# Ordering a Conformer block by list scheduling on estimated times, with attention started on the first keys

## Chip, cores and metric

One NeuronCore of a Trainium2 chip runs the whole kernel. The metric is device time in microseconds (us). Each run also has a profile, whose span (first to last instruction) is some 2 to 3 us shorter than the device time of the same run. Stages below are in span time.

## The reference, cut to what matters

`B, T, D, K, H = 2, 4000, 144, 5, 4`, so a head has 36 elements. All inputs and the output are bf16.

```python
h = _silu(_layernorm(x) @ w_ff1a) @ w_ff1b           # 144 -> 576 -> 144
x = x + 0.5 * h
q, k, v = split(_layernorm(x) @ w_qkv)               # 4 heads of 36
att = softmax(q k^T * 36**-0.5) v                    # 4000 x 4000, full
x = x + att @ w_o
a, b = split(_layernorm(x) @ w_pw1);  h = a * _sigmoid(b)
c = sum over 5 taps of hp[:, i:i+T, :] * dw[i]       # depthwise, along T
x = x + _silu(c) @ w_pw2
h = _silu(_layernorm(x) @ w_ff2a) @ w_ff2b
return _layernorm(x + 0.5 * h)
```

## The kernel before

Tokens are cut into 16 chunks of 500 (8 for each batch), a chunk into 4 blocks of 125. The work of a chunk is a generator: `pre` (first feed-forward, then queries, keys and values), an attention epilogue, `post1` (output projection and gated linear unit) and `post2` (convolution, second feed-forward, final norm, store). Attention is 32 groups (batch, chunk of queries, pair of heads), each over 32 key tiles: 1024 exps of 125x1000 on ScalarE, each between score matmuls (`emit_S`) and output matmuls (`emit_O`). A program order for all engines is fixed when the kernel is built. Semaphores order the engines at run time, and an engine runs its own instructions in order, so a matmul that was placed too early holds every matmul behind it.

The order comes from three simple rules. The front drains all of `pre` for the first batch, four chunks at a time, before any attention; in attention a pump lets background generators go on by a token rate for each engine; the tail drains what is left.

```python
def ln(c, to_bf=True):                       # a norm works on the whole chunk
    s = yield from lnp.take()
    for i in range(NB):
        op("dve", "bn_stats", ST[0:TB, s, i, :], X[0:TB, c * NB + i, :], ...)
    yield
    for i in range(NB):
        op("dve", "bn_aggr", MV[0:TB, s, i, :], ST[0:TB, s, i, :], ...)
    op("pool", "tensor_scalar", RS[0:TB, s, :, 1], MV[0:TB, s, :, 1], LN_EPS, None, op0=ALU.add, ...)
    op("pool", "tensor_tensor", RS[0:TB, s, :, 0], RS[0:TB, s, :, 1], NHALF[0:TB, :], op=ALU.pow, ...)
    yield
    yield
    for i in range(NB):
        op("dve", "tensor_scalar", XN[0:TB, s, i, :], X[0:TB, c * NB + i, :], MV[...], RS[...], ...)
# ...
drain([pre(all_banks, 0, True), first()] + [pre(all_banks, c, True) for c in range(1, CPB)], 4)
bg = Banks([6, 7])                           # PSUM banks of the background during attention
pump = Pump({"pe": 0.35 * CLUMP, "dve": 0.75 * CLUMP, "act": 0.25 * CLUMP})
# ...
def post2_thread(b):                         # one chunk after the other
    for c in range(b * CPB, (b + 1) * CPB):
        while c not in u_done or (c + 1 < (b + 1) * CPB and c + 1 not in u_done):
            yield
        yield from post2(bg, c)
# ...
for n in range(len(its)):
    if n + 1 < len(its):
        emit_S(n + 1)
    emit_exp(n)
    release_held()                           # tanh gates, behind the exp
    emit_pending(n, 2)
    pend.append(n)
    if n % CLUMP == CLUMP - 1:
        pump.slot(cap=3)
# ...
drain(pump.threads, 8)
```

Silu is the ScalarE function only in the front. During attention and in the tail it is built from Tanh (ScalarE) and one multiply (VectorE), so that the function table of the exps stays loaded.

The softmax here doesn't subtract the row's maximum and nothing guards it: scores larger than these inputs give would overflow.

Of the kernel before, what the change touches and what calls it, by code (L numbers as in the profile page):

```python
# [23 lines left out]
class Op:  # L24
    __slots__ = ("eng", "name", "a", "k", "idx", "deps", "clock", "inc", "waits", "cnt", "q")


class Rec:



    ENGS = ("pe", "act", "dve", "pool", "sp")

    def __init__(self, nc):
        self.nc = nc
        self.ops = []
        self.n = {}
        self.hist = {}
        self.qs = {}
        self.cost = {e: 0.0 for e in self.ENGS}  # L40

    def op(self, eng, name, *a, r=(), w=(), q=None, cost=0.0, **k):
# [10 lines left out]
        for key in w:  # L53
            h = self.hist.setdefault(key, ([], []))
            o.deps += [(d, False) for d in h[0] + h[1] if d is not o]
            if h[1] and not (len(h[1]) == 1 and h[1][0] is o):
                self.hist[key] = ([o], [])
            else:
                h[0].append(o)
        self.ops.append(o)  # L60
        self.cost[eng] += cost
        return o

    def finish(self, group_qs=()):
        eng_clock = {e: {} for e in self.ENGS}
        qtotal = {l: n for l, n in self.n.items() if l.startswith("q:")}
        for o in self.ops:
            clk = eng_clock[o.eng]
            need = {}
            for d, raw in o.deps:  # L70
                lane = d.eng if d.q is None else "q:" + d.q
                if d.q is None and d.eng == o.eng and (d.eng == "pe" or not raw):
                    continue
                if d.q is None and d.eng == o.eng and o.q is not None:
                    continue
                if clk.get(lane, -1) >= d.idx:
                    continue
                if lane not in need or need[lane].idx < d.idx:
                    need[lane] = d
# [52 lines left out]
class Banks:  # L132
    def __init__(self, ids):
        self.free = list(ids)

    def take(self):
        while not self.free:
            yield
        return self.free.pop(0)

    def give(self, i):
        self.free.append(i)


def bass_standalone__conformer_family_zipformer__speech_kernel(
# [22 lines left out]
    op = R.op  # L168

# [3 lines left out]
    NS, NXT, NTH, NHT = 6, 5, 6, 3  # L173
    X = sb("X", [NBLK, D])
    XN = sb("XN", [NS, NB, D])
    ST = sb("ST", [NS, NB, 6], F32)
    MV = sb("MV", [NS, NB, 2], F32)
    RS = sb("RS", [NS, NB, 2], F32)
    NHALF = sb("NHALF", [NB], F32)
# [6 lines left out]
    NPT = 6  # L186
    OLAG = 3
    CLUMP = 2
# [4 lines left out]
    U = sb("U", [2, T + 4])  # L193
    SW = sb("SW", [2, 2, CH])
    IDENT = sb("IDENT", [128])
    IDF = sb("IDF", [128], F32)
    WA1 = sb("WA1", [2, FF])
# [21 lines left out]
    def load(eng, q, dst, src, w):  # L219
        op(eng, "dma_start", dst, src, q=q, w=w)  # L220
# [14 lines left out]
    load_x("sp", 1)  # L235
    load("act", "w1", WQKV[0:HD, :, :], kh(w_qkv), ["WQKV"])
    for c in range(2, CPB):
        load_x("sp", c)
    load("act", "w2", WO[0:HD, :, :], kh(w_o), ["WO"])
    load("act", "w2", WP1[0:HD, :, :], kh(w_pw1), ["WP1"])  # L240
    load("act", "w2", WP2[0:HD, :, :], kh(w_pw2), ["WP2"])
    load("act", "w2", DWR[0:KCONV, :], dw, ["DWR"])
    load_ff("act", "w2", WA2, WB2, w_ff2a, w_ff2b, "W2")
    for c in range(CPB, NCH):
        load_x("sp", c)

    op("pool", "memset", IDENT[:, :], 0.0, w=["ID0"])
# [3 lines left out]
    op("dve", "tensor_copy", IDF[:, :], IDENT[:, :], r=["ID"], w=["IDF"])  # L251
# [3 lines left out]
    op("dve", "memset", WB2[0:64, 4, :], 0.0, w=[("W2", "b", 2)])  # L255

    def setup_qk():
        for Wt, nm, o0 in ((WQ, "WQ", 0), (WK, "WK", D)):
            for k in range(2):
                op("dve", "tensor_copy", Wt[0:HD, k, :, 0:DH],  # L260
                   WQKV[0:HD, k, o0:o0 + D].rearrange("p (h d) -> p h d", h=H), r=["WQKV", nm + "0"], w=[nm])

    def va_init(b):
        blks = slice(b * NKT, (b + 1) * NKT)
        op("pool", "memset", VA[:, blks, :, DH + 1:64], 0.0, w=[("VA0", b)])
        op("pool", "memset", VA[:, blks, :, DH:DH + 1], 1.0, w=[("VA1", b)])

    va_init(0)
    va_init(1)
    op("pool", "memset", U[:, :, 0:2], 0.0, w=["U0"])  # L270
    op("pool", "memset", U[:, :, T + 2:T + 4], 0.0, w=["U0"])

    def setup_dw(banks):
        bk = yield from banks.take()
        for k in range(2):
            op("pe", "transpose", PSH[0:HD, bk, k * 8:k * 8 + KCONV], DWR[0:KCONV, k * HD:(k + 1) * HD],
               IDENT[0:KCONV, 0:KCONV], r=["DWR", "ID"], w=[("ps", bk)])
        yield
# [4 lines left out]
        yield  # L283
        for k in range(2):
            for i in range(KCONV):
                op("dve", "tensor_scalar", DG[0:HD, k, i, :], IDENT[0:HD, 0:HD], DWT[0:HD, k, i:i + 1], None,
                   op0=ALU.mult, r=["DWT", "ID"], w=["DG"])


    lnp, xtp, thp, htp, swp, anp = (Banks(range(n)) for n in (NS, NXT, NTH, NHT, 2, 2))  # L290

    def xkeys(c):
        return [("X", c, i) for i in range(NB)]

    def ln(c, to_bf=True):
        s = yield from lnp.take()
        for i in range(NB):
            op("dve", "bn_stats", ST[0:TB, s, i, :], X[0:TB, c * NB + i, :], r=[("X", c, i)], w=[("ST", s, i)],
               cost=0.25)
        yield  # L300
        for i in range(NB):
            op("dve", "bn_aggr", MV[0:TB, s, i, :], ST[0:TB, s, i, :], r=[("ST", s, i)], w=[("MV", s)], cost=0.12)
        op("pool", "tensor_scalar", RS[0:TB, s, :, 1], MV[0:TB, s, :, 1], LN_EPS, None, op0=ALU.add,
           r=[("MV", s)], w=[("VE", s)], cost=0.3)
        op("pool", "tensor_tensor", RS[0:TB, s, :, 0], RS[0:TB, s, :, 1], NHALF[0:TB, :], op=ALU.pow,
           r=[("VE", s), "NHALF"], w=[("RS", s)], cost=1.0)
        yield
        yield
        for i in range(NB):
            op("dve", "tensor_scalar", XN[0:TB, s, i, :], X[0:TB, c * NB + i, :], MV[0:TB, s, i, 0:1],  # L310
               RS[0:TB, s, i, 0:1], op0=ALU.subtract, op1=ALU.mult, r=[("X", c, i), ("MV", s), ("RS", s)],
               w=[("XN", s)], cost=0.14)
        yield
        return s

    def tr(banks, src, rk, free):

        s = yield from xtp.take()
        bk = yield from banks.take()
        dst = PSH[0:HD, bk, :].rearrange("p (k i n) -> p k i n", k=2, i=NB)  # L320
        for k in range(2):
            for i in range(NB):
                op("pe", "transpose", dst[:, k, i, 0:TB], src[:, i, k * HD:(k + 1) * HD], IDENT[0:TB, 0:TB],
                   r=[rk, "ID"], w=[("ps", bk)], cost=0.06)
        free()
        yield
        op("dve", "tensor_copy", XT[0:HD, s, :, :].rearrange("p k (i n) -> p k i n", i=NB), dst[:, :, :, 0:TB],
           r=[("ps", bk)], w=[("XT", s)], cost=0.6)
        banks.give(bk)
        yield  # L330
        return s

    def ln_tr(banks, c):
        s = yield from ln(c)
        return (yield from tr(banks, XN[0:TB, s, :, :], ("XN", s), lambda: lnp.give(s)))

    def residual(banks, c, mm, scale, rk, cost):

        for g in range(2):
            bk = yield from banks.take()  # L340
            for i in (2 * g, 2 * g + 1):
                terms = mm(i)
                for t, (l, rh) in enumerate(terms):
                    op("pe", "matmul", PSV[0:TB, bk, (i % 2) * D:(i % 2 + 1) * D], lhsT=l, rhs=rh, start=t == 0,
                       stop=t == len(terms) - 1, r=rk, w=[("ps", bk)], cost=0.06)
            yield
            ks = [("X", c, 2 * g), ("X", c, 2 * g + 1)]
            xa = X[0:TB, c * NB + 2 * g:c * NB + 2 * g + 2, :]
            op("dve", "scalar_tensor_tensor", out=xa, in0=PSV[0:TB, bk, 0:2 * D].rearrange("p (i d) -> p i d", i=2),
               scalar=scale, in1=xa, op0=ALU.mult, op1=ALU.add, r=[("ps", bk)] + ks, w=ks, cost=0.37)  # L350
            banks.give(bk)
        yield

    held = []
    hold = [False]

    def tanh_gate(bk, rows, done=None):
        t = yield from thp.take()

        def emit():  # L360
            op("act", "activation", TH[0:rows, t, :], PSV[0:rows, bk, 0:CH], ACT.Tanh, bias=0.0, scale=0.5,
               r=[("ps", bk)], w=[("TH", t)], cost=0.47)
            if done:
                done()

        if hold[0]:
            held.append(emit)
        else:
            emit()
        return t  # L370

    def release_held():
        while held:
            held.pop(0)()

    def ff(banks, c, s, WA, WB, nm, silu):
        h = yield from htp.take()
        pend = []

        def flush():  # L380
            if pend:
                bk, t, m = pend.pop(0)
                op("dve", "scalar_tensor_tensor", out=HT[:, h, m, :], in0=TH[:, t, :], scalar=1.0,
                   in1=PSV[:, bk, 0:CH], op0=ALU.add, op1=ALU.mult, r=[("TH", t), ("ps", bk)], w=[("HT", h)],
                   cost=0.6)
                banks.give(bk)
                thp.give(t)
# [326 lines left out]
```

## Time and profile before

| quantity | before |
|---|---|
| device time, median of 3 | 1250.53 us (1247.25 to 1250.77) |
| span of the profiled run, mean granted clock | 1247.4 us, 0.927 |
| front, until the first exp | 133.6 us |
| attention, first exp to the end of the last | 1042.2 us |
| tail, end of the last exp to the end | 71.6 us |

First the profile page of before: busy time, and the busy share in 40 slices of the span, in tenths. PEclk is TensorE's granted clock, in tenths of full speed.

```profile
PE 987.3 (79%) x10722; PEld 377.0 (30%) x10722; DVE 535.6 (43%) x1596; ACT 1041.1 (83%) x1250; POOL 109.2 (9%) x173
...
DVE  6567333444353544444434343434333333333354
ACT  2221799999999998999999998999999999999711
...
PEclk9756799999999998999999988999999999999855
```

ScalarE is at 90% or more only between the first slices and the last three; in those slices the clock is 0.5 to 0.9. Next, the same run by stage, the view of busy time in given stretches (start:end, length, busy us of each engine with its instructions, clock, DMA share, GB/s):

```profile
core 0: us, PE busy (x) PEld busy (x) DVE busy (x) ACT busy (x) POOL busy (x), PEclk, DMA share, GB/s
0.00:44.00 44.00, 23.53 (x132) 13.98 (x132) 24.90 (x91) 12.12 (x20) 13.03 (x21) 1.00 0.25 75
44.00:98.00 54.00, 46.02 (x230) 27.60 (x231) 34.71 (x123) 9.39 (x16) 10.10 (x16) 0.53 0.00 1
98.00:133.60 35.60, 28.08 (x147) 16.45 (x145) 27.36 (x85) 3.90 (x6) 5.04 (x8) 0.58 0.00 1
133.60:1176.00 1042.40, 851.70 (x10046) 297.25 (x10042) 412.10 (x1189) 1004.26 (x1189) 73.45 (x116) 0.98 0.01 3
1176.00:1247.40 71.40, 37.96 (x178) 21.68 (x178) 36.54 (x112) 11.46 (x20) 7.59 (x12) 0.54 0.02 7
```

In the front no engine is full, and TensorE runs at about half clock for two stretches, which makes its matmuls look busy for twice as long. (The 1.00 of the first row is not to be trusted: 18 wide matmuls from 28.15 us on took 7.71 us there, 0.43 each, which is the half-clock speed. The clock's record begins only at 38.7 us in this run. What lies before it counts as full clock in the listed means, so before's 0.927 is too high.) In attention ScalarE is the limit: an exp follows another after 0.895 us and a tanh takes 0.477 us of its time, so 1024 exps and 165 tanh are 916.5 + 78.7 = 995 us of the stage's 1042.2. The other 47 us I call stalls. 36 us of them are gaps that the trace lists. (0.895 is the mean over repeats with no listed gap between them; the median repeat is 0.884, so the border between work and stall is not sharp.)

One stall of attention in before's timeline (start, us, engine, operation, idle before it and its releaser):

```profile
423.42 0.68 DVE L121 TENSOR_TENSOR OTF<-PS,OTA 128x500 f32<-128x500 f32 x1
...
424.15 0.74 PEld L121 LDWEIGHTS PS<-IDF,OTF 128*125 128x125 f32 x4 [1.63 <-DVE OTF L121]
...
425.95 1.05 PE L121 MATMUL PS<-QT,KT 64*64 64x500 bf16 x8
...
426.63 1.90 ACT L121 ACTIVATE PT<-PS 125x1000 bf16<-125x1000 f32 x2 [2.04 <-PE PS L121]
```

The transposes of an epilogue stood in TensorE's order ahead of scores. They waited 1.63 us for VectorE's OTF; the scores behind them came late; the next exp waited 2.04 us. The wait is put down to TensorE, but it begins with an operand of VectorE. It is not the only cause: the granted clock was 0.50 from 424.4 to 427.8 us, so the transposes and the scores (8 in 1.05 us) were slow as well.

Finally the tail in before's chain of waits (the work that ended last, in order of time). Bare "PE PS" entries are merged matmuls.

```profile
1197.77 4.40 PE PS L121 x10
...
1202.81 0.68 DVE SW L121
...
1210.73 4.36 PE PS L121 x10
...
1223.21 1.18 DVE SW L121 x2
...
1231.63 4.36 PE PS L121 x10
```

The chain runs through the second half of `post2` twice: SW, the gated convolution, is ready for the one chunk at 1202.8 and for the other only at 1223.2, after the first chunk's whole second feed-forward. The 4.36 us entries are ten wide matmuls of 500 columns at half clock.

### The profile page before, as it was taken

The page shows a single profiled execution, that of the slowest core. Times are in us where ns is not written, and L with a number is a line of the kernel's source. Part 1 is how long each engine was busy: PE and PEld are TensorE (multiplying, and loading weights), DVE is VectorE, ACT ScalarE, POOL GpSimd, SP SyncE. Part 2 cuts the span into 40 slices and gives each one's busy share as a digit, 9 for nine tenths or more (in the row PEclk, how much of TensorE's full clock was granted, in tenths as well). Part 3 has the DMA queues.
Part 4 walks back from the last instruction along what each step waited for, and adds up shares of the span by engine and source line. Part 5 has one row for each costly group of instructions (what it writes and reads, how often), then busy time and mean ns, then how long its engine had stood idle before and what let it go on. Part 6 is the DMA issues. An engine that isn't in the chain of part 4 may idle for free.

```text
span 1247.4 us, 24613 instructions
## 1 busy us (share of the span) xinstructions
PE 987.3 (79%) x10722; PEld 377.0 (30%) x10722; DVE 535.6 (43%) x1596; ACT 1041.1 (83%) x1250; POOL 109.2 (9%) x173
## 2 busy tenths in 40 slices
PE   3888787878888888888877788887877777878754
PEld 2545222223232323233322232332322222222322
DVE  6567333444353544444434343434333333333354
ACT  2221799999999998999999998999999999999711
POOL 4121000000010100010000000000000000000011
PEclk9756799999999998999999988999999999999855
DMA  3000000000000000000000000000000000000000
GB/s 105 1 1 1 1 2 1 1 2 1 2 2 6 1 2 6 1 1 6 1 6 1 6 6 1 6 1 6 6 1 6 1 6 1 6 1 6 1 5 10
DMA packets 6430, 7.14 MB, mean 6 GB/s; under 512 B 1746, under 2 KB 6322, under 8 KB 6322
## 3 DMA queue, kind: packets, MB, share of 16 engines
q1 hardware_dynamic: 4160, 4.61, 1.1%
q8 instruction: 84, 1.38, 0.5%
q10 hardware_dynamic: 2162, 0.96, 0.3%
q14 instruction: 24, 0.20, 0.1%
HBM read 3.26 MB, written 2.30 MB: 4 GB/s over the span
## 4 chain that ended last, share of the span: by engine, by line
ACT 63%; PE 24%; DVE 9%; POOL 1%; issue 1%; DMA 1%; ACTq 0%; POOLq 0%; DVEq 0%
ACT PT L121 58%; PE PS L121 24%; ACT TH L121 5%; DVE OTF L121 2%; DVE OTA L121 2%; POOL RS L121 1%; DVE ST L121 1%; DVE XN L121 1%; DMA WB<-in_w_ff2b_dram 1%; DVE KT L121 1%; DVE VA L121 0%; DVE X L121 0%; ACTq L121 0%; DVE XT L121 0%; DVE MV L121 0%
## 5 line engine op out<-in xcount | busy, mean ns | idle before, releaser
L121 ACT ACTIVATE PT<-PS 125x1000 bf16<-125x1000 f32 x1024 | 949.4, 1059 | 51.0 <-PE PS L121 49.6
L121 PE MATMUL PS<-QT,KT 64*64 64x500 bf16 (+1 forms) x4096 | 412.3, 398 | 151.6 <-ACT PT L121 141.4
L121 PE MATMUL PS<-PT,VA 61*64 61x500 bf16 (+1 forms) x4096 | 385.4, 377 | 0.5 <-ACT PT L121 0.4
L121 PEld LDWEIGHTS PS<-QT,KT 64*64 64x64 bf16 (+1 forms) x4096 | 113.8, 104 | 532.3 <-ACT PT L121 495.5
L121 ACT ACTIVATE TH<-PS 128x500 bf16<-128x500 f32 (+1 forms) x184 | 115.9, 637 | 58.6 <-PE PS L121 57.6
L121 DVE SCALAR_TENSOR_TENSOR HT<-TH,PS 128x500 bf16<-128x500 bf16 x120 | 80.6, 674 | 146.5 <-ACT TH L121 146.5
L121 PEld LDWEIGHTS PS<-PT,VA 61*64 61x64 bf16 (+1 forms) x4096 | 119.9, 108 | 18.0 <-issue 4.7
L121 DVE SCALAR_TENSOR_TENSOR X<-PS,X 125x288 bf16<-125x288 f32 x128 | 58.5, 457 | 143.4 <-PE PS L121 143.1
L121 POOL TENSOR_SCALAR RS<-MV 125x4 f32<-125x4 f32 x80 | 18.4, 231 | 1126.4 <-DVE MV L121 1126.4
L121 DVE COPY XT<-PS 72x1000 bf16<-72x1000 bf16 x80 | 53.4, 676 | 140.9 <-PE PS L121 140.3
L121 PE MATMUL PS<-XT,WA 72*128 72x500 bf16 x320 | 107.0, 449 | 8.1 <-DVE HT L121 4.7
L121 DVE TENSOR_SCALAR XN<-X,MV,RS 125x144 bf16<-125x144 bf16 x320 | 79.4, 312 | 40.2 <-POOL RS L121 40.2
L121 ACT ACTIVATE HT<-PS 128x500 bf16<-128x500 f32 x40 | 22.8, 588 | 78.7 <-PE PS L121 78.7
L121 POOL TENSOR_TENSOR RS<-RS,NHALF 125x4 f32<-125x4 f32 x80 | 83.4, 1043 | 6.7
L121 DVE BATCH_NORM_STATS2 ST<-X 125x6 f32<-125x144 bf16 x320 | 76.4, 327 | 0.0
L121 PE MATMUL PS<-IDENT,XN 125*72 125x125 bf16 x512 | 47.3, 247 | 30.5 <-DVE XN L121 30.4
L121 PE MATMUL PS<-WB,HT 128*125 128x144 bf16 x640 | 60.3, 255 | 5.4 <-DVE HT L121 3.6
L121 PEld LDWEIGHTS PS<-WB,HT 128*125 128x125 bf16 x640 | 54.6, 161 | 21.7 <-issue 8.7
L121 PEld LDWEIGHTS PS<-IDENT,XN 125*72 125x72 bf16 x512 | 37.2, 130 | 51.2 <-DVE XN L121 34.8
L121 DVE SCALAR_TENSOR_TENSOR U<-TH,PS 72x500 bf16<-72x500 bf16 x32 | 32.3, 1009 | 43.3 <-ACT PT L121 27.0
L121 DVE COPY OTA<-PS 128x500 f32<-128x500 f32 x32 | 21.7, 679 | 64.7 <-PE PS L121 64.7
L121 PE MATMUL PS<-IDF,OTF 128*125 128x128 f32 x128 | 23.4, 307 | 29.4 <-DVE OTF L121 29.4
(46 smaller groups left out, 487.0 us busy)
## 6 DMA issues: line engine op xcount, KB each, us to landing
X<-in_x_dram SPq DMA_DIRECT2D x16, 140.6 KB
out_dram<-XN SPq DMA_DIRECT2D x16, 140.6 KB
WA<-in_w_ff1a_dram ACTq DMA_DIRECT2D x1, 162.0 KB
WA<-in_w_ff2a_dram ACTq DMA_DIRECT2D x1, 162.0 KB
WB<-in_w_ff1b_dram ACTq DMA_DIRECT2D x1, 144.0 KB
WB<-in_w_ff2b_dram ACTq DMA_DIRECT2D x1, 144.0 KB
WQKV<-in_w_qkv_dram ACTq DMA_DIRECT2D x1, 121.5 KB
WP<-in_w_pw_dram ACTq DMA_DIRECT2D x1, 81.0 KB
```

The costliest lines, as they stand in the source:

```text
L121: ins = getattr(eng, o.name)(*o.a, **o.k)
```

## The change

The intent is to use the same operations in a better order. Each recorded operation now has a cost, and the recorder keeps an estimated start and end for it. At each step the generator whose next piece can start first goes on (list scheduling), against the estimated start of the next scores. Attention begins as soon as all first feed-forwards of batch 0 and the keys of chunk 0 are done; the projections of chunks 1 to 7 run inside the first attention group. Norms, transposes and residuals work on half chunks. Silu is the ScalarE function in the front and, new, in the tail. 36 dummy matmuls run at the start to raise the clock. Two `post2` series run side by side. Smaller parts: U has a layout with a contiguous write (1.01 us before for one), at the price of 9 matmuls instead of 5 for one convolution half; value-tile clearing moves from large GpSimd operations to small VectorE ones (in before, VectorE's cast of an identity matrix took 7.11 us beside them; the Trainium skill, "SBUF — State Buffer", section "Who interferes with whom", says that a VectorE cast in one of its two-port modes and a GpSimd operation block each other; the trace fits, with 7.07 us of clearing on GpSimd beside the cast, but doesn't show the mode); the matrices for the convolution are made after the front and not at its start; ScalarE shares copies in front and tail; the late weights load from another queue; the output is stored in halves.

The diff, cut to its core (cuts are marked):

```diff
+    LAT = dict(pe=0.2, act=0.2, dve=0.12, pool=0.08, sp=2.0)
...
+        start = self.free[eng]
+        for d, raw in o.deps:
+            if d.eng != eng or d.q is not None or (raw and eng != "pe"):
+                start = max(start, d.done)
...
+        self.free[eng] = start + cost
+        o.done = start + cost + self.LAT[eng]
...
+class Sched:
+    def best(self, window=0.15):
+        c = [(self.start_of(th), th) for th in self.threads]
+        c = [(t, th) for t, th in c if t is not None]
...
+        lim = min(t for t, _ in c) + window
+        return next((t, th) for t, th in c if t <= lim)
...
+    NWARM = 36
+    for i in range(NWARM):
+        op("pe", "matmul", PSV[:, i % 8, 0:CH], lhsT=DUM[:, 0:128], rhs=DUM[:, 0:CH], ...)
...
-    def ln(c, to_bf=True):
-        s = yield from lnp.take()
-        for i in range(NB):
+    def ln(c, g):
+        u = yield need("dve", xnp)
+        for i in range(2):
...
-               out=U[0:HD, hf, 2 + cc * CH:2 + (cc + 1) * CH].rearrange("p (n i) -> p n i", i=NB),
+        op("dve", "scalar_tensor_tensor", out=U[0:HD, cc, hf, :, 1:1 + TB],
...
+        silu = mode["tail"]
+        kids = S.spawn(conv(c, z, hf, silu) for hf in range(2))
...
-    drain([pre(all_banks, 0, True), first()] + [pre(all_banks, c, True) for c in range(1, CPB)], 4)
+    while len(ff1_done) < CPB or 0 not in kv_done:
+        t, th = S.best()
+        S.run(th)
+    att_banks = set(range(6))
+    banks.restrict([6, 7])
...
+    while n_e < NIT:
+        a = s_start(n_s) if n_s < NIT else R.free["pe"]
+        t, th = S.best()
+        if th is not None and (a is None or t < a or (th.req[0] == "act" and t < a + 0.05)):
+            S.run(th)
+            if mode["front"] and len(kv_done) == CPB:
+                mode["front"] = False
+                S.add(setup_dw())
+                S.add(series(g for c in range(CPB, NCH) for g in (ff1(c, False), pre2(c))))
+                for par in range(2):
+                    S.add(series(post2(c) for c in range(par, NCH, 2)))
+            continue
+        if n_s < NIT:
+            emit_S(n_s)
+            n_s += 1
+        if n_s >= 2 or n_s == NIT:
+            emit_exp(n_e)
+            emit_pending()
...
-    drain(pump.threads, 8)
+    mode["tail"] = True
...
+    while S.threads:
+        t, th = S.best()
+        S.run(th)
```

## The prediction

> What bounds the kernel now. The timeline of ScalarE and the busy time by windows show three stages. Front, 0 to 133.6 us, until the first exp: ScalarE is busy 2 to 3 us in 10, VectorE 6; chunks go through their norms in lockstep, TensorE waits for VectorE and its granted clock falls to 0.50 from about 46 to 90 us and again later. Attention, 133.6 to 1176 us: ScalarE is the limit. An exp repeats every 0.895 us, a tanh takes 0.48 us of its time, so 1024 exps are 916 us and some 164 tanh 79 us; the other 47 us are stalls (ScalarE's listed gaps sum to 36 us, all released by TensorE). The long ones (2.0 us at 427, 2.4 at 495, 2.4 at 761) come where TensorE, in order, sat behind a background matmul whose VectorE operand was late; there the clock shows 0.50 too. Tail, 1176 to 1247 us: 71 us of one dependent chain for the last chunks, one after the other, clock about 0.5.
>
> What changes.
> 1. Front. Only the first feed-forward of eight chunks and chunk 0's keys must end before attention. By the order of instructions VectorE has about 43 us of work up to the first query copy, costed with the trace (statistics 0.22, aggregate 0.09, normalise 0.25, residual 0.46, half copy about 0.36 us). It starts near 10 us, when the query-key-value weight lands (9.5 us before). Half chunks and readiness order keep TensorE fed, dummy matmuls warm it; warm it needs about 4 us a chunk (0.21 us per wide matmul, as seen at 41 us), cold 8. First exp: estimate 55 us (80 if cold). Gain about 78 us.
> 2. The projections of chunks 1 to 7 now run inside the first attention group, on two PSUM banks. Eight bank uses a chunk at about 1.5 us each make 6 us a chunk, near the 37 us that 32 exps and 17 evacuation copies on ScalarE take. Cost: 8 us of copies plus about 12 us of stalls.
> 3. Steady attention. Background work is placed where its inputs should be ready; norms and residuals in halves. I expect head-of-line stalls to fall from 47 to about 15 us. Exps and tanh stay (168 tanh by the order): about 997 us.
> 4. Tail. The last two chunks side by side, halved chains, Silu instead of tanh plus multiply, eight banks. Two table loads more at 1.28 us (the trace's duration; the Trainium skill, "ScalarE: Activation LUTs", section "What ACT_TABLE_LOAD costs", says the same). Still about half clock: 44 us instead of 71.
>
> Sum: 55 + 997 + 8 + 12 + 15 + 44 = 1131 us span, plus 3 us between span and device time: about 1134 us, 9% faster. Range 1105 to 1170. Chances: faster by over 2% 0.96, within 2% 0.03, slower 0.01.
>
> What would show it. First exp at 45 to 65 us; clock near 1 in the front; exp repeat unchanged at 0.895 us; ScalarE gaps of about 12 us in the first 40 us of attention and under 20 us after; last exp to end about 44 us.
>
> What would make it wrong. The order is fixed by estimated times with little slack: an under-estimated VectorE or GpSimd duration makes TensorE wait in order and delays scores by that much, hundreds of times. The dummies may not keep the clock up: in the front now, 72-row matmuls ran back to back at 0.42 us from 22 to 36 us without getting faster, so the front could take 80 us. Two banks could starve the first group.

## More of the kernel before

Waits in before (what waited for what: us in total, times, longest) include the front and the tail. The third is TensorE's, for OTF, the operand of an epilogue's transposes:

```profile
ACT TH L121 <- PE PS L121: 57.6, 33, 11.9
ACT PT L121 <- PE PS L121: 49.6, 43, 22.3
...
PE PS L121 <- DVE OTF L121: 29.4, 29, 1.6
```

## The result, and the profile after

The changed kernel took 1156.85 us (median of four runs: 1147.39, 1151.92, 1161.77, and 1178.51, which counts as slow because it is over 1.5% above the fastest). The ratio to before is 0.923, with an interval of 0.916 to 0.931. Ratios here and below are the mean time of one kernel's fast runs over that of the other's of the same rounds, so not quite the ratio of the medians that I quote. The prediction was 1134 us with a range of 1105 to 1170.

| stage, us of span | before | after | difference |
|---|---|---|---|
| front, until the first exp | 133.6 | 58.2 | -75.4 |
| attention | 1042.2 | 1038.6 | -3.6 |
| tail | 71.6 | 48.8 | -22.8 |
| whole span (mean clock) | 1247.4 (0.927) | 1145.6 (0.977) | -101.8 |

So three quarters of the gain lie in the front and nearly all of the rest in the tail. The profiled run was the fastest of the four; that is a point of its own, taken up below.

The profile page of after, with the same columns:

```profile
PE 959.3 (84%) x10886; PEld 367.5 (32%) x10886; DVE 526.4 (46%) x1657; ACT 1060.9 (93%) x1290; POOL 153.9 (13%) x359
...
DVE  5975655666766643342424520433424241424324
ACT  3789999999999999999999999999999999999942
...
PEclk8999999999999999999999999999999999999966
```

The stages of after, busy time in given stretches. VectorE and TensorE are nearly full from 28 to 58.2 us, which they never were in before's front:

```profile
0.00:16.00 16.00, 12.24 (x52) 5.15 (x52) 7.47 (x44) 2.45 (x3) 5.07 (x17) 1.00 0.48 136
16.00:28.00 12.00, 10.17 (x44) 5.46 (x45) 7.19 (x36) 6.59 (x11) 5.67 (x13) 0.57 0.26 92
28.00:58.20 30.20, 30.02 (x302) 21.01 (x300) 27.34 (x115) 23.64 (x46) 12.11 (x26) 1.00 0.01 2
58.20:1096.80 1038.60, 876.09 (x10322) 316.29 (x10322) 463.54 (x1387) 1015.08 (x1210) 121.39 (x281) 1.00 0.01 3
1096.80:1145.60 48.80, 30.80 (x168) 19.61 (x168) 20.85 (x79) 13.14 (x22) 9.66 (x23) 0.59 0.02 6
```

The same waits in after:

```profile
ACT PT L135 <- PE PS L135: 10.3, 38, 1.5
...
ACT TH L135 <- PE PS L135: 6.2, 13, 1.1
...
PE PS L135 <- DVE OTF L135: 2.2, 3, 1.6
```

TensorE's wait for OTF, which stood in its order ahead of scores, is listed 29 times in before (there are 32 groups) and 3 times in after: this is what the new order took out of attention. All its listed waits for VectorE there went from 38 to 26 us, as shorter ones for HT rose from 5 to 18.

Attention became only 3.6 us shorter because work moved into it. The same sum as before reads: 916.5 us of exps, 80 us of 168 tanh, and new 7.7 us of 17 copies for the projections of chunks 1 to 7. That leaves about 34 us of stalls, against 47. The stalls fell by 13, the work grew by 9.

The longest stall of attention in after's timeline looks different from before's:

```profile
562.20 0.41 PE L135 MATMUL PS<-QT,KT 64*64 64x500 bf16 x4 [0.41 <-ACT PT L135]
...
563.58 0.63 PE L135 MATMUL PS<-QT,KT 64*64 64x500 bf16 x4 [0.97 <-ACT PT L135]
...
564.97 1.21 PE L135 MATMUL PS<-IDF,OTF 128*125 128x128 f32 x4
...
566.80 1.90 ACT L135 ACTIVATE PT<-PS 125x1000 bf16<-125x1000 f32 x2 [1.48 <-PE PS L135]
```

TensorE did not wait for VectorE here. It waited 0.97 us for ScalarE, because it had nothing else to do; from 564 to 566 us its granted clock was 0.50, the transposes came in that stretch, and the exp was 1.48 us late. It is the only such stretch in after's attention.

The tail in after's chain of waits:

```profile
1113.29 9.54 PE PS L135 x44
1122.85 0.59 ACT SW L135
...
1127.08 6.46 PE PS L135 x28
1133.57 0.47 DVE X L135
```

The 44 merged matmuls hold the convolutions of both last chunks, and SW (now written by ScalarE's Silu) appears once. The second feed-forward appears once as well.

### The profile page after: what moved, and what is told of

It is laid out like the page before. It is cut to its first block, busy times and chain, and to the rows that moved or that the text cites. A ratio compares the mean times of both kernels' runs of the same rounds, so it can differ in the third digit from the quotient of the medians.

```text
span 1145.6 us, 25298 instructions
## 1 busy us (share of the span) xinstructions
PE 959.3 (84%) x10886; PEld 367.5 (32%) x10886; DVE 526.4 (46%) x1657; ACT 1060.9 (93%) x1290; POOL 153.9 (13%) x359
## 4 chain that ended last, share of the span: by engine, by line
ACT 68%; PE 23%; DVE 5%; POOL 2%; issue 1%; DMA 1%; ACTq 0%; POOLq 0%; DVEq 0%
ACT PT L135 61%; PE PS L135 23%; ACT TH L135 6%; DVE HT L135 1%; POOL RS L135 1%; DVE XN L135 1%; DVE U L135 1%; DMA WQKV<-in_w_qkv_dram 1%; DVE ST L135 0%; DVE X L135 0%; ACT QT L135 0%; DVE MV L135 0%; DVE VA L135 0%; DVE OTF L135 0%; ACT XT L135 0%
## 5 line engine op out<-in xcount | busy, mean ns | idle before, releaser
L135 ACT ACTIVATE PT<-PS 125x1000 bf16<-125x1000 f32 x1024 | 953.5, 1071 | 12.6 <-PE PS L135 10.3
L135 POOL TENSOR_SCALAR RS<-MV 125x2 f32<-125x2 f32 x160 | 34.9, 218 | 883.6 <-DVE MV L135 883.0
L135 POOL TENSOR_TENSOR RS<-RS,NHALF 125x2 f32<-125x2 f32 x160 | 113.9, 712 | 13.4
L135 ACT ACTIVATE TH<-PS 128x500 bf16<-128x500 f32 (+1 forms) x170 | 107.1, 630 | 6.3 <-PE PS L135 6.2
L135 DVE SCALAR_TENSOR_TENSOR HT<-TH,PS 128x500 bf16<-128x500 bf16 x110 | 72.9, 672 | 78.9 <-ACT TH L135 78.8
L135 PE MATMUL PS<-XT,WA 72*128 72x500 bf16 x320 | 93.7, 398 | 9.3 <-DVE HT L135 7.0
L135 DVE SCALAR_TENSOR_TENSOR X<-PS,X 125x288 bf16<-125x288 f32 x128 | 57.2, 448 | 57.0 <-PE PS L135 56.7
L135 DVE COPY XT<-PS 72x500 bf16<-72x500 bf16 x143 | 57.7, 413 | 43.6 <-PE PS L135 43.1
L135 PE MATMUL PS<-IDENT,XN 125*72 125x125 bf16 x512 | 50.9, 228 | 11.7 <-DVE XN L135 9.3
L135 PEld LDWEIGHTS PS<-WB,HT 128*125 128x125 bf16 x640 | 45.5, 141 | 29.4 <-DVE HT L135 17.3
L135 PEld LDWEIGHTS PS<-IDENT,XN 125*72 125x72 bf16 x512 | 33.7, 115 | 55.9 <-DVE XN L135 32.2
L135 DVE SCALAR_TENSOR_TENSOR U<-TH,PS 72x500 bf16<-72x500 bf16 x32 | 21.5, 671 | 60.0 <-ACT PT L135 30.5
L135 PE MATMUL PS<-U,DG 72*72 72x250 bf16 (+3 forms) x288 | 44.1, 305 | 4.5 <-POOL U L135 3.8
L135 PEld LDWEIGHTS PS<-XT,WA 72*128 72x128 bf16 x320 | 23.4, 101 | 69.0 <-DVE HT L135 29.7
```

What stands on the lines that cost most here:

```text
L135: ins = getattr(eng, o.name)(*o.a, **o.k)
```

## Experiments

What was open: is the gain one of order and shorter chains, or of TensorE's clock, which rose from 0.927 to 0.977? What do the separate parts give? And why do the runs of one kernel differ by 1%? All kernels gave a correct result. Times are medians, with the ratio to before's fast runs of the same rounds and its interval. Before took 1247.4 to 1253.7 us in all of these rounds. Span and stages are of the one profiled run, so differences of a few us between stages can be the clock's; stages of the same instructions differed by up to 0.9 us in the front and 14.7 in attention.

| run | median us | ratio (interval) | span | first exp | attention | tail |
|---|---|---|---|---|---|---|
| after, again | 1153.32 | 0.9239 (0.9209 to 0.9268) | 1161.2 | 59.1 | 1053.3 | 48.8 |
| nowarm | 1151.24 | 0.9218 (0.9198 to 0.9237) | 1147.7 | 57.2 | 1041.7 | 48.8 |
| keysfirst | 1167.70 | 0.9343 (0.9296 to 0.9391) | 1174.4 | 91.0 | 1033.9 | 49.5 |
| bridge | 1150.39 | 0.9200 (0.9181 to 0.9219) | 1146.8 | 53.9 | 1044.1 | 48.8 |
| tanhtail | 1162.88 | 0.9302 (0.9280 to 0.9323) | 1156.7 | 58.9 | 1039.4 | 58.4 |
| fullnorm | 1151.76 | 0.9214 (0.9197 to 0.9230) | 1150.6 | 61.3 | 1037.0 | 52.2 |
| lat0 | 1225.91 | 0.9804 (0.9779 to 0.9829) | 1222.6 | 61.9 | 1110.5 | 50.2 |
| lat2 | 1165.03 | 0.9327 (0.9304 to 0.9349) | 1162.9 | 58.1 | 1053.9 | 50.9 |
| warmtail | 1149.29 | 0.9189 (0.9172 to 0.9205) | 1148.0 | 58.3 | 1045.6 | 44.1 |
| trans | 1152.09 | 0.9212 (0.9199 to 0.9226) | 1152.3 | 58.9 | 1043.4 | 50.1 |
| bwarm (before, with dummies) | 1226.68 | 0.9816 (0.9788 to 0.9845) | 1225.9 | 109.4 | 1045.5 | 71.0 |
| best | 1144.93 | 0.9154 (0.9132 to 0.9177) | 1147.0 | 57.3 | 1045.7 | 44.1 |

### again: the changed kernel once more

No edit.

> The changed kernel as it is, once more, to see what its spread of 1147 to 1179 us is. In the four runs on record the time rises as the mean granted clock falls (0.977: 1147, 0.971: 1152, 0.960: 1162, 0.943: 1179). Theory A (clock): the spread is TensorE at half clock in stretches whose start depends on the run; then 5 more runs fall on the same line, about 0.9 us for each thousandth of clock. Rival B (disturbance from outside): times vary at the same clock.

Six more runs took 1150.49 to 1162.99 us, median 1153.32. The time follows the clock: with the four runs above, a mean clock of 0.977, 0.973, 0.971, 0.963, 0.960, 0.959 and 0.943 goes with 1147.4, about 1150.5, 1152, 1159, 1162, 1163 and 1178.5 us, close to 0.9 us for each 0.001 of clock. The profile happened to take a long one. Busy time in stretches of this run:

```profile
58.00:60.00 2.00, 0.85 (x12) 0.56 (x8) 1.96 (x8) 1.99 (x3) 0.00 (x0) 1.00 0.00 0
60.00:62.00 2.00, 1.88 (x10) 0.32 (x10) 0.35 (x2) 1.85 (x3) 0.00 (x0) 0.51 0.00 0
62.00:70.00 8.00, 8.00 (x49) 2.65 (x49) 4.51 (x15) 3.91 (x5) 1.86 (x4) 0.50 0.01 2
70.00:80.00 10.00, 10.00 (x63) 3.38 (x63) 5.97 (x26) 5.56 (x8) 2.87 (x6) 0.50 0.00 0
```

At the change from front to attention TensorE idles for 1.27 us, waiting for the first exp, which itself waits for a table load of 1.28 us. In this run the clock then fell and stayed at half for 27 us, although TensorE shows no more idle time. TensorE had 110 instructions in 62 to 80 us, against 176 in the other profile; ScalarE starves (busy for 9.5 us of the 18, against 15.7), and attention is 14.7 us longer. The first profile of after has the same idle 1.27 us and no such stretch. So the same instructions give either, and a lucky profile is not a description of the kernel.

### nowarm: no dummy matmuls at the start

```diff
-    NWARM = 36
+    NWARM = 0
```

> The 36 dummy matmuls at the start are taken out, nothing else. In the trace of the changed kernel the clock rose at about 7 us under the dummies and had fallen again by 17 us, one us before the first wide matmul, which then ran at 0.42 us up to 27 us. Theory A: the dummies buy nothing, the time stays within 3 us of the changed kernel's and the clock in 18 to 27 us is 0.50 in both. Rival B: they keep a state that makes the clock rise sooner at 27 us; without them the front stays at half clock as in the kernel before, first exp at 70 to 80 us and the time 15 to 20 us longer.

The dummies buy nothing: 1151.24 us and a first exp at 57.2, against 1153.32 and 59.1. They do raise the clock, but between 12 and 18 us TensorE is busy for only 2 us, waiting for normalised tokens, and the clock fell at 17.2 us, one us before the wide matmuls. (The scheduler's order changes a little without them, so this is not a pure removal.)

### bridge: small dummies in that hole

```diff
+    bridge, BR = [5], 4
+    del banks.free[7]
...
+        if bridge[0] > 0:                    # after each of the first 5 half-chunk transposes
+            bridge[0] -= 1
+            for _ in range(BR):
+                op("pe", "matmul", PSV[:, 7, 0:256], lhsT=DUM[:, 0:128], rhs=DUM[:, 0:256], ...)
```

> Four more dummy matmuls (256 columns) after each of the first five transposes of the front, into a bank kept free for them; the order of everything else is the same. If the clock falls at 17 us because TensorE is nearly idle from 12 to 18 us (theory A), it now stays at 1.0 through 30 us, the first 16 wide matmuls run at 0.21 us instead of 0.42, the first exp comes 3 to 5 us earlier and the run-to-run spread shrinks. Rival B: 72-row matmuls themselves let the clock fall (in the kernel before they ran back to back at 0.42 us for 14 us); then the clock falls anyway and nothing is gained.

The first exp came at 53.9 us instead of 58.2. The first wide matmuls in the timeline, of after and then of bridge:

```profile
18.24 6.83 PE L135 MATMUL PS<-XT,WA 72*128 72x500 bf16 x16 [0.97 <-ACT XT L135]
```

```profile
18.23 3.55 PE L135 MATMUL PS<-XT,WA 72*128 72x500 bf16 x16 [0.52 <-ACT XT L135]
```

Sixteen matmuls take 6.83 us at half clock (cold) and 3.55 us at full clock (warm); one of 500 columns follows another after 0.42 and 0.21 us. The Trainium skill, "TensorE: Matmul & The Clock Gate", Part 1, gives N/1.2 ns cold and N/2.4 + 2.5 ns warm for N columns, by estimate 417 and 211 ns for 500; the trace agrees. The four microseconds were won in the front, and the median is 1150.39. In this profile they were spent again: its attention has five half-clock stretches of 3.4 us, one at its start and four in which an exp is 1.2 to 1.5 us late (at 438, 629, 882 and 946 us).

### keysfirst: all keys of batch 0 before any attention

```diff
-    while len(ff1_done) < CPB or 0 not in kv_done:
+    while len(ff1_done) < CPB or len(kv_done) < CPB:
...
     banks.restrict([6, 7])
+    mode["front"] = False
+    S.add(setup_dw())
+    S.add(series(...))                       # batch 1 and post2, moved here from the loop
```

> Attention waits for the keys of all eight chunks, as before the change; list scheduling, half chains, Silu stay. Theory A: the front's gain comes from two parts; packed by the list scheduler the whole front with all projections ends at about 88 us instead of 133, and starting attention early gains only the rest, 30 us, of which it pays 8 us of copies and about 9 us of stalls back in attention: this run is 12 to 18 us slower than the changed kernel. Rival B: the early start is the main source; this run loses 40 us or more.

This undoes one part, the early start of attention. The first exp came at 91.0 us, so the rest of the change (list scheduling with its half chains, shared copies and the smaller parts) takes the front from 133.6 to 91.0, and the early start takes it on to 58.2. In time the early start is worth less than these 33 us: at an equal mean clock of 0.973, keysfirst took 1160.5 and again 1150.6, about 10 us; the medians differ by 14. The projections are not saved, only moved to where ScalarE and TensorE are wanted by attention, whose stage is shorter by 4.7 us in keysfirst. The clock blurs the stage figures: in the profiled run of keysfirst, 67 to 98 us ran at half clock.

### bwarm: the kernel before, its order kept, with dummies in the front

```diff
+        if banks is all_banks:               # in tr(), ahead of the transposes
+            for _ in range(6 if calls[0] == 0 else (14, 1, 1, 0)[calls[0] % 4]):
+                op("pe", "matmul", PSV[:, bk, 0:CH], lhsT=DUM[:, 0:128], rhs=DUM[:, 0:CH], ...)
+            calls[0] += 1
```

> This is the kernel before, with dummy matmuls in its front alone: 14 before the first transposes of each later batch of chunks, where TensorE idles about 4 us for the norms, one or two elsewhere; the order of everything else stays. It asks why the front with all eight chunks' projections took 133.6 us in the kernel before and 91.0 us under the list scheduler. In the kernel before, the clock was 0.50 for some 89 us of the front. Theory A (packing): norms in lockstep and VectorE's copies set the pace, the half clock adds only where TensorE ran back to back; with the clock near 1.0 the front shrinks to 110 to 120 us, so that the clock is less than half of the 43 us. Rival B (clock): the half clock is most of it; the front shrinks to 105 us or less and the time by 28 us or more. If the dummies do not hold the clock up the run tells nothing.

This is the rival by itself: better clock, same order. The first exp came at 109.4 us instead of 133.6, and the time fell to 1226.68. From 44 to 98 us the clock was 0.91, where before had 0.53, but 19 us of the front from there on (53 to 63 and from 101 us) were still at half clock. So of the 42.6 us between before's front and that of keysfirst, a partly warm clock under the old order gives 24.2, more than half. The remaining 18 us are not all packing. The first instructions of TensorE on the tokens, in before and then in after:

```profile
15.37 0.28 PE L121 MATMUL PS<-IDENT,DWR 5*72 5x5 bf16 x2 [15.37 <-DMA WB<-in_w_ff2b_dram]
18.82 2.88 PE L121 MATMUL PS<-IDENT,XN 125*72 125x125 bf16 x24 [3.17 <-DVE XN L121]
```

```profile
12.07 0.41 PE L135 MATMUL PS<-IDENT,XN 125*72 125x125 bf16 x4 [0.29 <-DVE XN L135]
```

Before's order puts the transposes of the convolution's weight first. They wait for the late weights until 15.37 us, VectorE waits 3.68 us for them, and the first chunk's transposes start at 18.82 (19.06 in bwarm). In after this set-up comes behind the front, and they start at 12.07. So up to 7 of the 18 us belong to this move, which no run undid alone; that the other 11 are packing is inferred and not shown.

### lat0 and lat2: wrong estimates

```diff
-    LAT = dict(pe=0.2, act=0.2, dve=0.12, pool=0.08, sp=2.0)
+    LAT = dict(pe=0.0, act=0.0, dve=0.0, pool=0.0, sp=2.0)     # lat0
+    LAT = dict(pe=0.4, act=0.4, dve=0.24, pool=0.16, sp=2.0)   # lat2
```

> The order of work is made with the estimated latencies between engines (0.08 to 0.2 us) set to zero, all else the same: every operand is then believed ready 0.1 to 0.4 us too early per step. Theory A (the prediction's worry): TensorE then sits in order behind late operands, stalls in attention rise from about 30 to 45 us or more, and the clock dips more often. Rival B: ScalarE's queue of two score banks absorbs errors of that size: within 5 us of the changed kernel.

> The estimated latencies between engines are doubled (0.4, 0.4, 0.24, 0.16 us), all else the same. With them at zero attention took 1110 us instead of 1039. Theory A: the order needs estimates that are not too short, and the present ones are already long enough: attention stays within 6 us of 1039 us. Rival B: longer is better still, since a few waits of 0.2 to 0.5 us remain per chunk: attention falls to 1030 us or less. Rival C: the estimates must hit, too long is as bad as too short: attention rises by 15 us or more.

LAT is the estimate of the time from the end of an operation until another engine may start on its result. Only the order of instructions depends on it. With zero, attention took 1110.5 us, 72 more than in after, and three quarters of the whole gain over before are gone. The direction had been expected, the size not. Waits in lat0, against 10.3, 6.2 and 2.2 us in after:

```profile
ACT TH L135 <- PE PS L135: 41.4, 60, 1.6
ACT PT L135 <- PE PS L135: 33.9, 75, 1.4
...
PE PS L135 <- DVE OTF L135: 23.5, 30, 1.6
```

No wait of ScalarE is long, the longest takes 1.6 us and the mean of these 135 is 0.56, but they come back with each background chunk: TensorE, in order, stands before a matmul that the plan believed ready. Its own wait for OTF is back 30 times, and its listed waits for VectorE in attention sum to 79 us, against 26 in after and 38 in before. With LAT doubled, attention took 1053.9 us, 15 more than in after, but no more than in again (1053.3): part of it is the clock. At a nearly equal clock lat2 is 7 to 11 us longer than again (1170.3 against 1163.0 us at 0.959, 1164.7 and 1165.0 at 0.968 against 1154.3 at 0.969). Why is not shown; that background pieces come too late is one reading. So both errors cost, and the margin near the right value is a few tenths of a microsecond.

### tanhtail: tanh and multiply in the tail

```diff
-        silu = mode["tail"]
+        silu = False
...
-        yield from ff(c, s, WA2, WB2, "W2", mode["tail"], store)
+        yield from ff(c, s, WA2, WB2, "W2", False, store)
```

> Only Silu in the tail is undone: the last two chunks use tanh and the VectorE multiply again; everything else, copies on ScalarE in the tail too, stays. The tail of the changed kernel is 48.8 us in every trace. Theory A: Silu saves only the multiply at the end of each gate, about 0.7 us twice on the chain, and one table load of 1.28 us is hidden in a wait; the tail becomes 50 to 52 us and the time about 2 us longer. Rival B: Silu is the main reason for the 22 us that the tail lost; then the tail is 60 us or more.

The tail took 58.4 us, 9.6 more than with Silu. It lies between the two values that were expected. Not all of it is Silu's: the clock was 0.50 in nearly the whole of this tail (56.1 of 58.4 us, against 39.5 of 48.8 in after), and the matmuls of the two second feed-forwards took 3.9 us longer in all. One of the four runs, 1183.22 us, was slow. The scheduler's order of the two chunks also changed. Silu saves a VectorE multiply behind each gate, at the price of table loads: there are four in after and two in before, of 1.28 us each. The Trainium skill, "ScalarE: Activation LUTs", section "What ACT_TABLE_LOAD costs", gives 1283 ns for one, and the trace agrees.

### fullnorm: norms over whole chunks again

```diff
-    def ln(c, g):
-        for i in range(2):
+    def ln(c):
+        for i in range(NB):                  # four blocks, one pow for all, cost=0.95
...
-        kids = S.spawn(ln_tr(c, s, g) for g in range(2))
+        kids = S.spawn([ln_tr(c, s)])        # behind both residual halves
```

> Only the half-chunk norm chains are undone: one chain of four blocks for statistics, power and normalise, as before the change (transposes, residuals and stores stay in halves). A half chain took 0.5 + 0.24 + 0.22 + 0.71 + 0.55 us in the trace, a whole one 0.93 + 0.36 + 0.23 + 1.04 + 1.00. Theory A: it matters only in front and tail, where each whole chain on the dependent path costs about 1.3 us more: tail 52 to 54 us, first exp 2 to 4 us later, attention unchanged within 4 us, in all 5 to 9 us slower. Rival B: halves matter throughout, because they spread VectorE's work: attention stalls rise by 10 us or more. Rival C: halves cost more GpSimd time (149 us against 102) and undoing them is no loss.

The half chains bring the first exp 3.1 us forward (2.2 against again) and shorten the tail by 3.4; the tail of trans, in the same order as after's, was itself 1.3 us longer than after's. The median is nevertheless the same, 1151.76 us, which is not what was expected: the clock of these four runs was higher (0.974 to 0.977, against 0.959 to 0.973 in again). At an equal clock of 0.977 the span is some 3 us longer (1148.6 and 1148.9, against the one run of 1145.6). The price of halves is GpSimd time: 153.9 us busy in after, 107.3 in fullnorm, as recorded. Two pow of half the width take 0.71 us each against 1.04 for the whole, and the small addition ahead of each is doubled too.

### warmtail and trans: dummies where the clock was seen to fall

```diff
+        if th.req[0] == "pe":                # warmtail: fill estimated holes of the tail
+            for _ in range(min(13, int((t - R.free["pe"] - 0.15) / 0.21))):
+                op("pe", "matmul", PSV[:, 0, 0:CH], lhsT=DUM[:, 0:128], rhs=DUM[:, 0:CH], ...)
```

```diff
+        if n_s == 2:                         # trans: while TensorE awaits the first exp
+            for _ in range(6):
+                op("pe", "matmul", PSV[:, 4, 0:CH], lhsT=DUM[:, 0:128], rhs=DUM[:, 0:CH], ...)
```

> Dummy matmuls fill TensorE's estimated gaps in the tail (47 before the last real matmul), nothing else changes. In all traces of the changed kernel the tail runs about 34 us at a granted clock of 0.50, with wide matmuls at 0.42 us. Theory A: the half clock costs the dependent chain about half of its long matmul runs (3.55 + 8.8 + 4.35 us of them, now at 0.42 us each): the tail shrinks from 48.8 to 40 to 43 us. Rival B: the dummies delay real work in order as much as the clock gains: tail 47 us or more.

> Six dummy matmuls stand before the third score group, where TensorE waits 1.27 us for the first exp behind the table load; the order of everything else is that of the changed kernel. One run of the unchanged kernel showed the clock at 0.50 from 60 to 88 us there, and was 15 us longer. Theory A: that stretch is what spreads the changed kernel's times and the short wait starts it; six runs now stay within 1146 to 1153 us, with no run of 1157 or more (4 of 10 so far). Rival B: the stretch has another cause, or the matmuls at half clock keep it going however it starts; about 4 in 10 runs are again at 1157 us or more.

In warmtail the tail fell from 48.8 to 44.1 us, somewhat short of the 40 to 43 expected, and its half-clock time from 39.5 to 10.2 us; ten wide matmuls of the first chunk's second feed-forward took 2.29 us, 4.35 in after. In trans, four fast runs took 1151.32 to 1154.2 us; none reached 1157, which 4 of the 10 runs of the unedited kernel did, and the profile has no stretch at 60 us. That fits the idle 1.27 us as the start of the long stretch, but four runs are too few to show it: with a share of 4 in 10, four good runs come by chance one time in eight (0.6 to the fourth power is 0.13). And the fillers are not needed for it: bridge and warmtail keep the 1.27 us idle, nowarm and fullnorm 0.96, and none of their 16 runs reached 1157 either. The median of trans is no better than that of again, and its profile's attention had five short stretches elsewhere.

### best: bridge, trans and warmtail together

The edits above, with at most 53 dummies in the tail.

> The dummies of three runs together: after the first transposes, before the third score group, and in the gaps of the tail (53 there). If their gains add up: first exp at 54 us, no long stretch at half clock at the start of attention, tail 44 us: about 58.2 - 53.9 + 48.8 - 44.1 = 9 us less than the changed kernel's clean run, 1138 to 1144 us. If the clock dips elsewhere instead, as it did in the run with dummies only in the front (four dips in attention of about 2 us each), 1145 us or more.

It beats both kernels: 1144.93 us, five runs from 1140.7 to 1148.88. The run with the highest clock (0.989) was the fastest. The profiled run had one half-clock stretch of 14 us at 90 and four short ones in attention, and its first exp came at 57.3, not at the 54 expected, as the clock fell from 19.5 to 26.3 us in spite of the fillers. So the front's gain was mostly missing once more. The median is at the upper edge of what was expected. The named reason, stretches elsewhere, is seen in the one profile; it does not tell about the other four runs.

## Why the prediction was right

The time was 23 us above the predicted 1134 in the first four runs and 19 in the next six, well inside the range, and the mechanism was the predicted one. Term by term, against the profile of after:

| term of the sum | predicted us | measured us |
|---|---|---|
| first exp | 55 | 58.2 |
| exps, tanh and copies on ScalarE | 997 + 8 | 1004 |
| stalls in the first group and after | 12 + 15 | 34 in all |
| tail | 44 | 48.8 |
| span | 1131 | 1145.6 |

- **Front.** The early start and the fuller engines of 28 to 58 us came as said. That the clock holds was half right: it was 0.57 from 16 to 28 us, and the dummies at the start, credited in the prediction with keeping TensorE warm, give nothing (nowarm). So that the front took 58 us, and not the 80 named for a cold one, is not owed to the reason given; without the dummies it took 57.2. A hole of a few microseconds behind them undoes them; filling the hole gives 4.3 us (bridge).
- **Attention.** The exp's repeat stayed at 0.895 us. ScalarE stood idle for 6.1 us in the first 40 us (predicted 12) and, by stretches up to 1090, for 17.4 us after that (predicted under 20). The predicted 27 us of stalls were 34. Of these 23.5 are gaps, fewer than predicted; some 10 are repeats a little longer than 0.895. Those were 11 before (47 less 36) and hardly fell, while the prediction's sum had the whole 47 fall to 15.
- **Tail.** The prediction named the parts and summed them to 27 us; 22.8 came. Silu gives 9.6 (tanhtail, of which up to 4 can be the clock) and half chains up to 3.4 (fullnorm). The other 9.8 us are a subtraction: the chain of waits passes the second feed-forward once instead of twice, but no run undid that alone, and the nine-matmul convolution works against it.
- **The mis-sized term.** The sum assumed a clock near 1 outside the tail. That holds in the profiled run (attention at 1.00) but not in a usual one: half-clock stretches, mostly of 3.4 us in attention and once of 27 us, add up to 15 us from run to run (0.977 to 0.959 of clock). The 14.6 us between 1131 and 1145.6 are small misses of each term; the further 6 to 9 us between the best run and the medians are this clock.
- **The named risk.** An order fixed by estimates is fragile, and lat0 shows how much: 72 us for two tenths of a microsecond that the plan leaves out. The estimates of the change are good enough (both zero and double are worse), so the risk did not come true.

Order against clock, then: bwarm shows that a partly warm clock in the front alone is worth 23 us of time in the old order, and keysfirst together with the stage table shows that the new order and its set-up get further. They are coupled: TensorE was busy 30.0 of 30.2 us at full clock at the end of after's front, where before's had gaps and half clock.

When the clock falls can be read from the traces in part. It changes only on a grid of 3.413 us, which lies differently in each run. In the attention of the fourteen profiles, from its second window on, TensorE was busy for at most 0.62 of the grid's window before 55 of 63 falls, and in only 57 of the 4110 windows of full clock that no fall followed. All 45 short stretches after the first group, in after and the runs with its scheduler, begin 2 to 4 exps into a group of 32. There the code holds the new group's output matmuls back until the epilogue has read the old sums, and TensorE runs short. So the place of a stretch is the program's, and which groups have one can depend on how the grid lies. No run tested this, and near the border it doesn't decide: at the first exp a window busy for 0.66 was followed by a fall in again, and windows of 0.67 in after and 0.63 in warmtail were not. What stays open is what ends a stretch: bridge's at 55.9 us lasted 3.4 us and again's at 60.0 us lasted 27.3, with TensorE busy all the time in both.

## What to carry to other kernels

Where engines run in order, rank background work by when its inputs will be ready, with durations and hand-over times read from the trace; here too short a hand-over estimate cost 72 us and one too long some 10. Start the limiting engine as soon as its first inputs exist, but count the moved work, which comes back in its stage: here 33 us of earlier start gave 10 to 14. Put filler matmuls into the holes right before wide matmuls, not at the beginning, and judge a kernel by several runs with their clocks and not by one profile.

## What the Trainium skill lacked or had wrong

- "TensorE: Matmul & The Clock Gate", Part 1, says that an array that is kept busy for about 3.4 us gets the full clock. Here 18 wide matmuls of 72 rows ran back to back in 7.71 us in before, still cold, and TensorE shows 18.0 of 18 us busy at a clock of 0.50 from 62 to 80 us in again. Busy time as the profile shows it is not enough; of what is counted the page says only, in Part 4, that transposes do not count in the same way.
- The same page, "HAM oscillation", gives "no PE-idle gaps >~3.4µs" as the rule. Here the clock fell after less: TensorE's busy time from 562 to 564 us in after was 0.83 of 2.00 us, with single gaps of about 1 us, and half clock followed for 3.4 us. A later section of the page tells of short idle times, frequent enough, that make the clock swing, but gives no share; here it was about 0.62 busy, as counted above. That the stretches have the length of the page's window, 3413 ns, agrees.
- The same page calls the cold start run-variable, and says nothing of stretches that come later in some runs only: ten runs of the changed kernel had mean clocks of 0.943 to 0.977 and times of 1147.4 to 1178.5 us.
- "ScalarE: Activation LUTs", section "What ACT_TABLE_LOAD costs", gives 186 ns + 0.833 ns an element for an operation and an overlap of about 93 ns between two. For 1000 elements that is a repeat of 926 ns, an estimate from these figures; the exps here, which read PSUM, repeat every 895 ns in the mean and 884 in the median.
- No page gives the time of a pow on GpSimd for a few elements per partition: as recorded, 0.71 us for two and 1.04 us for four.
